# Two transformer layers on one core: where the second-stage weights are measured, and how many softmax units VectorE takes per head

## The chip, the cores and the metric

The kernel runs on one core of one Trainium2 chip. The metric is device time in microseconds, and the median of three runs of the kernel before is 1906.23 us (1905.84 to 1906.58). In this text PE is the matrix engine TensorE, DVE is VectorE, ACT is ScalarE, POOL is GpSimd and SP is SyncE.

## The reference

The input `x` has 2048 tokens of 448 features. Two layers with the same weights are run over it, and each layer is an attention block followed by a gated block, both with a layer norm ahead and a residual add behind:

```python
x = x + A(_layernorm(x))     # qkv = x @ wqkv; 16 heads of 28; softmax(q k^T * 28**-0.5) v; @ wo
x = x + B(_layernorm(x))     # h = sigmoid(x @ w_gate) * (x @ w_up); h @ w_down, 1792 hidden
x = x + A(_layernorm(x))
x = x + B(_layernorm(x))
```

All arrays are float32.

## The kernel before, in words

The kernel is one instruction stream per engine, in the order in which the program emits it; each engine takes its instructions strictly in that order and waits at the head of its queue. Matrix products use pairs of float16 numbers, a high part and the rest. To choose the power of two by which a weight is scaled before it is split so, the kernel first needs the sum of squares of that weight over all its elements.

**Projections (`project`).** Tokens are four blocks of 512. For each block, `qk` makes seven tiles of 128 rows of queries and keys (11 matmuls each, in four rotating accumulators), and `vals` makes four tiles of values. Each `qk` tile is left by ACT (high part, squares) and DVE (low part, maximum of squares), and is stored to `qk_scr` in DRAM by a DMA from the SP queue. Work of the next blocks hangs between the tiles, in lists named `fill` and `along_values`: a block is normalised (`norm`, DVE and POOL), turned in 32 x 32 pieces into a tile `xs` (`squares`, DVE), stored to DRAM (`store`), read back in another order (`gather`), and split into high and low parts (`ready`, ACT and DVE). Block 2 and block 3 go this way in layer 0.

**Attention (`attend`).** A head has 16 chunks of 128 keys, a chunk has 4 units (128 keys by 512 queries), so a layer has 1024 units. Most units are taken three at a time as a group: PE makes the scores, ACT takes the exponential of the 128 x 1536 tile in one instruction, and PE multiplies the result with the values (`mix`, some two groups later). A few units a head go another way, and are called aside: PE makes the scores in a bank of their own (`score_aside`), and DVE works out the exponential with a polynomial, ten instructions a unit. `ASIDE` gives, for one, two or three such units a head, the chunk at which each is begun and the chunk in which it is used. `FEW` gives the number of units aside for each head of layer 0; in layer 1 all heads have three. The bank that a head's asides use is the accumulator bank of the head before it: `finish` of that head (DVE turns the accumulator, divides it and splits it, six instructions) has to have read it first.

**Preparation (`Prepare`).** During the attention of layer 0, the weights of the output projection and of the gated block are put into the form that the later stages read. Steps hang behind chunks of the attention: a list of (chunk, step) pairs is worked off by `along(c)` whenever `mix` has completed chunk c. First every weight is measured: a raw tile of up to 128 x 2048 float32 comes in by DMAs from the POOL queue, and DVE squares and adds it up (`measure`, `add`). There are twelve such tiles: `o` (`wo`), four `d` (`w_down`), seven `gu` (256 columns of `w_gate` and of `w_up`). Then `sizes` sums over partitions on POOL (`partition_all_reduce`) and makes the scales on DVE. Then come the splits: `o`, seven `w` steps (`w_down`) and fourteen `g`/`u` steps, each of them a read from the POOL queue, some 14 DVE instructions, and a DMA of the result to DRAM one step later. Each step issues the read of the next tile; the raw tiles rotate through two buffers, so a read waits until the step before has read its buffer. The DVE instructions of a step are not tied to the time of their chunk, only to their place in DVE's queue.

**Buffers.** `Slots` hands out 19 large tiles first in, first out: a tile that is given back goes to the end of the list, and its next owner waits until all its former readers, DMAs included, are done.

Of the kernel before, what the change touches and what calls it, by code (L numbers as in the profile page):

```python
# [19 lines left out]
P = 128  # L20
# [44 lines left out]


ASIDE = {1: ((6, 15, 1),), 2: ((4, 10, 3), (9, 15, 1)), 3: ((4, 9, 3), (8, 13, 1), (12, 15, 2))}
FEW = "2221212111111233"


TAIL = (0, 1, 3, 2, 5, 4, 6)
# [47 lines left out]
def interleaved_layers(ctx: ExitStack, tc: tile.TileContext, x_in, wqkv, wo, w_gate, w_up,  # L119
# [591 lines left out]
    def project(layer, wq, begun):  # L711
# [109 lines left out]
        if layer == 0:  # L821
            def scaled():
                b1.xn = big.get("xn", [P, TB, D])
                for j in range(TB):
                    b1.scale(j)

            def turned(kts):
                b1.turn_banks(6, kts)
                for j in range(TB):
                    b1.turn(j)  # L830
                b1.turned_high()
                b1.turned_low()

            fill = [idle, idle, lambda: b1.norm([0, 1]), lambda: b1.norm([2, 3]), idle, scaled]
            along_values = {0: lambda: (b1.parts(), turned([0, 1])),
                            1: lambda: (turned([2, 3]), big.put(b1.xn)),
                            2: lambda: (fin(), b2.norm()),
                            3: lambda: (b2.squares(), b2.store())}
        else:
            ones_of_values()  # L840
            fill = [idle, lambda: b1.ready(0, 1), lambda: b1.ready(2, 3), b2.norm,
                    lambda: b2.squares([0, 1]), sq(2, 2, 3), b2.store]
            along_values = {0: b3.norm, 1: lambda: (fin(), sq(3, 0, 1)()), 2: b2.gather,
                            3: sq(3, 2, 3)}
# [6 lines left out]
            fill = [idle, lambda: b2.ready(0, 1), lambda: b2.ready(2, 3), b3.store]  # L851
        fin = qk(1, b1, fill, None)
        vals(1, b1, {0: b3.gather, 2 if layer == 0 else 1: fin})
        fin = qk(2, b2, [idle, lambda: b3.ready(0, 1), lambda: b3.ready(2, 3)], None)
        fin = qk(3, blks[3], [], fin)
        if layer > 0:
            big.put(*wq.qk)
        else:
# [58 lines left out]

        return values, heads, last_values

    def true_maxima(h):  # L920

        hd = HeadOperands(h, "mx")
        hd.load()
        uid[0] += 1
        mx = cpool.tile([P, NT], F32, name=f"mx_{uid[0]}", tag="mx", bufs=2)
        mp = cpool.tile([P, 4], F32, name=f"mp_{uid[0]}", tag="mp", bufs=2)
        for t in range(NT):
            for g in range(NB):
# [12 lines left out]
        nc.sync.dma_start(g_scr[h].rearrange("c (t p) -> t c p", p=P), parts)  # L941
        hd.drop()


    class Prepare:


        def __init__(self):
            nc.vector.memset(sums[:, 3:7], 0.0)
            self.part = cpool.tile([P, 2], F32, name="part", tag="part", bufs=1)  # L950
            self.raws, self.packs = big.ring(2), big.ring(2)
            self.halves, self.half = None, 0
            tiles = [("o", 0)] + [("d", j) for j in range(4)] + [("gu", j) for j in range(7)]
            order = [(self.measure, what) for what in tiles] + [
                (self.split, what) for what in tiles[:1] + [("w", p) for p in range(NP)] + [
                    (w, p) for p in range(NP) for w in ("g", "u")]]
            self.read(*tiles[0])
            self.steps = deque()
            at = 6
            for i, (do, what) in enumerate(order):  # L960
                then = order[i + 1][1] if i + 1 < len(order) else None
                self.steps.append((at, lambda do=do, what=what, then=then:
                                   self.step(do, what, then)))
                at += ((5 if what[0] == "gu" else 4) if do == self.measure else
                       {"o": 5, "w": 8}.get(what[0], 7))
                if i == len(tiles) - 1:
                    self.steps.append((at, self.sizes))
            self.steps.append((at, self.end))
            self.pack = None
# [10 lines left out]
        def read(self, kind, j):  # L980
# [12 lines left out]
            elif kind == "w":  # L993
                for z in range(2):
                    r = slice((z * NP + j) * P, (z * NP + j + 1) * P)
                    nc.gpsimd.dma_start(self.view(self.next, kind)[:, z], w_down[r])
            elif kind in "gu":
# [7 lines left out]
            else:  # L1005
                n = self.count(j)
                nc.gpsimd.dma_start(self.view(self.next, kind)[:, 0:n, :],
                                    w_down[j * 512:j * 512 + n * P, :].rearrange(
                                        "(s p) n -> p s n", p=P))

        def count(self, j):
            return min(4, NF - 4 * j)

        def view(self, t, kind):
            if kind == "gu":
# [37 lines left out]
            nc.vector.tensor_copy(sums[:, m:m + 1], self.part[:, 0:1])  # L1053

        def measure(self, raw, kind, j):
            if kind == "o":
                self.add(3, raw[:, 0:4 * D])
            elif kind == "gu":
                self.add(4, raw[:, 0:1024])
                self.add(5, raw[:, 1024:2048])  # L1060
            else:
                self.add(6, raw[:, 0:self.count(j) * D])

        def sizes(self):
            nc.gpsimd.partition_all_reduce(size[:, 3:7], sums[:, 3:7], channels=P,
                                           reduce_op=ReduceOp.add)
            powers(3, 4, size[:, 3:7])
            both_back(1, 2, 3, 2.0 ** -23)
            both_back(2, 5, 6, 2.0 ** -22)
# [767 lines left out]
```

## Time and profile before

| what | value |
|---|---|
| median of three runs | 1906.23 us |
| the profiled execution's own time | 1904.97 us |
| its span, first to last instruction | 1903.2 us |
| granted TensorE clock | 1.000 |
| PE / PE weight loads busy | 1891.3 / 1365.4 us (99% / 72%) |
| DVE / ACT / POOL busy | 1391.6 / 1386.7 / 255.9 us (73% / 73% / 13%) |
| projections of layer 0 | up to 118.7 us |
| attention of layer 0 (first to last group's start) | 119.6 to 567.3 us, 333 ACT groups |
| gated block of layer 0, projections of layer 1 | to 1062 us |
| attention of layer 1 (first to last group's start) | 1063.1 to 1506.5 us, 326 ACT groups |
| gated block of layer 1 | to the end |

PE shows as busy nearly all the time, but the ends of matmuls are modelled in the profile, so that a PE that waits a little between matmuls also shows as busy. What limits a stage has to be read from the stage itself: in attention, from whether ACT's groups stand end to end. In a row of the timeline the columns are the start in us, the duration in us, the engine, the line of the kernel, the operation, the tile written and the tiles read, the shapes, the count, and in brackets the time the engine stood idle before and what ended it.

### The profile page before, as it was taken

The numbers are of one execution on the slowest core, as the hardware profiler recorded it, in microseconds if no ns is written. First come the engines' busy times: TensorE is split into PE (matmuls) and PEld (weight loads), VectorE is DVE, ScalarE is ACT, GpSimd is POOL, SyncE is SP. The second block draws the span as 40 slices with busy tenths as digits, with TensorE's granted clock in tenths as the row PEclk, the third lists the DMA queues.
The fourth block names the chain that finished last, engine by engine and source line by source line (L and its number), as shares of the span: only waits on it lengthen the run. The fifth ranks groups of instructions, "written<-read, shape, count | busy, mean of one in ns | idle before, by whom it ended". The sixth has DMA issues, their size and how long they took to land. (4 is left out here: it accounts for less than half of the span.)

```text
span 1903.2 us, 56306 instructions
## 1 busy us (share of the span) xinstructions
PE 1891.3 (99%) x24281; PEld 1365.4 (72%) x24281; DVE 1391.6 (73%) x2768; ACT 1386.7 (73%) x1772; POOL 255.9 (13%) x523
## 2 busy tenths in 40 slices
PE   9999999999999999999999999999999999999999
PEld 4455555555556789999954568777777767899998
DVE  7648798697886688787564487787778676887664
ACT  5569999999993556555344799999999745565541
POOL 2013312232102211222100000000000021121110
PEclk9999999999999999999999999999999999999999
DMA  5575554445213565646734321122121244566553
GB/s 175 166 208 159 153 165 138 129 139 159 91 64 106 179 220 226 225 190 226 255 109 128 94 52 44 34 51 52 30 48 53 69 132 152 215 243 232 210 206 141
DMA packets 107953, 269.79 MB, mean 142 GB/s; under 512 B 12894, under 2 KB 64222, under 8 KB 107568
## 3 DMA queue, kind: packets, MB, share of 16 engines
q0 software_dynamic: 32592, 162.18, 23.8%
q1 hardware_dynamic: 74768, 103.71, 19.4%
q8 instruction: 191, 3.13, 0.7%
q14 instruction: 66, 0.54, 0.1%
q10 hardware_dynamic: 336, 0.23, 0.0%
HBM read 207.88 MB, written 50.85 MB: 136 GB/s over the span
## 5 line engine op out<-in xcount | busy, mean ns | idle before, releaser
L1177 ACT ACTIVATE prob_s<-sc 128x1536 f32<-128x1536 f32 x659 | 892.0, 1485 | 6.6 <-PE sc L1162 6.4
L1213 PE MATMUL acc<-prob_s,val_s 128*32 128x256 f32 (+3 forms) x7754 | 579.7, 383 | 0.0
L1162 PE MATMUL sc<-qp_s 114*32 114x512 f16 x7896 | 565.5, 379 | 0.0
L578 PEld LDWEIGHTS <-gu_s 128*128 128x128 f16 x4368 | 426.8, 98 | 51.3 <-issue 3.8
L1162 PEld LDWEIGHTS <-qp_s 114*32 114x32 f16 x8192 | 288.2, 95 | 192.7 <-issue 94.5
L1213 PEld LDWEIGHTS acc<-prob_s,val_s 128*32 128x32 f32 x7754 | 297.9, 110 | 115.6 <-issue 8.6
L578 PE MATMUL chain<-xwide_s,gu_s 128*128 128x256 f16 x2016 | 248.0, 273 | 3.3 <-ACT two_q L1591 1.4
L1491 PE MATMUL dnp<-dn_s,hparts_s 128*128 128x224 f16 x2016 | 225.2, 259 | 0.0
L1491 PEld LDWEIGHTS <-hparts_s 128*128 128x128 f16 x2016 | 194.0, 98 | 4.5
L1564 ACT COPY one_q<-chain 128x256 f32<-128x256 f32 x224 | 82.3, 371 | 122.5 <-PE chain L578 122.0
L1193 DVE SCALAR_TENSOR_TENSOR power_q<-power_q,expo_q 128x512 f32<-128x512 f32 x222 | 153.7, 692 | 7.6
L1580 DVE TENSOR_TENSOR one_q<-side,one_q 128x512 f32<-128x512 f32 x112 | 72.2, 686 | 106.5 <-PE side L578 103.9
L578 PE MATMUL side<-xshort_s,gu_s 128*128 128x256 f16 x1120 | 140.6, 273 | 0.0
L563 PE MATMUL qkp<-xhl_s,wqk_s 128*128 128x512 f16 x616 | 138.0, 379 | 0.7 <-DVE xhl_s L542 0.3
L1378 POOL DMA_DIRECT2D gu_s<-gu_parts x104 | 56.2, 541 | 417.5 <-PE side L578 393.4
L563 PEld LDWEIGHTS <-wqk_s 128*128 128x128 f16 x616 | 60.0, 98 | 70.2 <-ACT wqk_s L231 1.1
L1242 DVE STREAM_TRANSPOSE oturned_q<-acc 128x512 f32<-128x512 f32 x32 | 22.9, 716 | 117.4 <-PE acc L1213 117.4
L578 PE MATMUL side<-xwide_s,gu_s 128*128 128x256 f16 x672 | 91.7, 273 | 0.0
L755 ACT ACTIVATE qkhl_q<-qkp 128x512 f16<-128x512 f32 x56 | 33.2, 593 | 74.5 <-PE qkp L563 72.9
L1444 ACT CAST hparts_s<-hsums_q 128x256 f16<-128x256 f32 (+1 forms) x136 | 65.1, 494 | 29.4 <-DVE hsums_q L1456 20.4
L1213 PE MATMUL acc<-power_q,val_s 128*32 128x256 f32 (+3 forms) x278 | 86.3, 393 | 0.0
L1591 ACT ACTIVATE one_q<-one_q 128x512 f32<-128x512 f32 x56 | 35.2, 629 | 64.6 <-DVE one_q L1580 64.6
(213 smaller groups left out, 2321.3 us busy)
## 6 DMA issues: line engine op xcount, KB each, us to landing
gu_s<-gu_parts POOLq DMA_DIRECT2D x104, 800.0 KB, 5.8
dn_s<-dn_parts POOLq DMA_DIRECT2D x42, 784.0 KB, 7.5
qp_s<-qk_scr SPq DMA_DIRECT2D x96, 224.0 KB
qk_scr<-qkhl_q SPq DMA_DIRECT2D x56, 256.0 KB
gu_parts<-pack_s POOLq DMA_DIRECT2D x14, 800.0 KB, 3.8
xt_scr<-xs_s SPq DMA_DIRECT2D x48, 224.0 KB
xraw_s<-xt_scr SPq DMA_DIRECT2D x12, 768.0 KB
qp_s<-qk_scr SPq DMA_DIRECT2D x64, 112.0 KB
```

Of the source, the lines that this page charges most:

```text
L563: nc.tensor.matmul(pm, w, x, start=(i == 0), stop=(i == len(terms) - 1))
L578: nc.tensor.matmul(pm, a, x, start=(first and i == 0), stop=(i == len(terms) - 1), skip_group_check=True)
L1162: nc.tensor.matmul(ps[32 * j:32 * j + 32, :], hd.k[:, keys], hd.q[:, qb * W:(qb + 1) * W], start=True, stop=True, tile_position=(0, 32 * j))
L1177: nc.scalar.activation(prob[:, 0:n, :], ps[:, 0:n, :], AF.Exp, scale=exp_scale)
L1193: nc.vector.scalar_tensor_tensor(p, p, c[k], y, op0=ALU.add, op1=ALU.mult)
L1213: nc.tensor.matmul(acc[qb * VC:(qb + 1) * VC, s], v[:, kc % TB, h, :], probs[c * NB + qb][:, s], start=(kc == 0 and a == 0), stop=(kc == N ...
L1378: queue.dma_start(self.gu[-1][m], gu_parts[p, m])
L1444: nc.scalar.copy(to[:, :, 0], a)
L1491: nc.tensor.matmul(pm, a[:, x, t], w[:, p, y], start=(begin and n == 0 and (j == 0 or alone)), stop=(n == 2), skip_group_check=True)
L1564: nc.scalar.copy(to, pm)
L1580: nc.vector.tensor_tensor(one[m], side[m], one[m], op=ALU.add)
L1591: nc.scalar.activation(out, v, AF.Sigmoid, scale=gate_scale)
```

## The change

Half of the measuring leaves the attention of layer 0. A new class `Measure` reads six of the twelve tiles (`o`, the four `d`, the first `gu`) by the POOL queue during the values of block 0 in layer 0's projections, and adds them up on DVE behind the last three `qk` tiles of block 2 and the first three of block 3; half of the `gu` tile goes to ACT. It holds one large tile for a scrap output, and up to six for the raw tiles. `Prepare` keeps six `gu` tiles, four chunks apart (five before). POOL's sum over partitions becomes a step of its own, `reduce`, and the DVE work that uses it, `sizes`, follows six chunks later. The splits stand further apart: 10 chunks for `w` (8 before), 9 for `g` and `u` (7 before), 4 after `o` (5 before); the first split of `w` now stands at chunk 40, the last step at chunk 227, and the end at 236 (66, 213 and 220 before). `FEW` gives two units aside to every head of layer 0 but the last, which has three: 33 in all (26 before), so 991 units go to ACT, in 331 groups (998 in 333 before). Head 14 had three before and has two; heads 3, 5 and 7 to 12 had one and have two.

```diff
-FEW = "2221212111111233"
+FEW = "2222222222222223"
...
-            along_values = {0: lambda: (b1.parts(), turned([0, 1])),
-                            1: lambda: (turned([2, 3]), big.put(b1.xn)),
-                            2: lambda: (fin(), b2.norm()),
-                            3: lambda: (b2.squares(), b2.store())}
+            tell = Measure()
+            along_values = {0: lambda: (b1.parts(), turned([0, 1]), tell.read(2)),
+                            1: lambda: (turned([2, 3]), big.put(b1.xn), tell.read(2)),
+                            2: lambda: (fin(), b2.norm(), tell.read()),
+                            3: lambda: (b2.squares(), b2.store(), tell.read())}
...
-        fin = qk(2, b2, [idle, lambda: b3.ready(0, 1), lambda: b3.ready(2, 3)], None)
-        fin = qk(3, blks[3], [], fin)
+        add = tell.add if layer == 0 else idle
+        fin = qk(2, b2, [idle, lambda: b3.ready(0, 1), lambda: b3.ready(2, 3), idle, add, add,
+                         add], None)
+        fin = qk(3, blks[3], [add, add, add], fin)
...
+    class Measure:
+        def __init__(self):
+            nc.vector.memset(sums[:, 3:7], 0.0)
+            self.part = cpool.tile([P, 2], F32, name="part0", tag="part", bufs=1)
+            self.junk = big.get("junk", [P, 2048], BF16)
+            self.to_read = deque([("o", 0)] + [("d", j) for j in range(4)] + [("gu", 0)])
+            self.rows = deque()
+
+        def read(self, n=1):
+            for _ in range(n):
+                kind, j = self.to_read.popleft()
+                t = big.get("raw", [P, 2048])
+                n = {"o": 4, "d": min(4, NF - 4 * j), "gu": 0}[kind]
+                v = t[:, 0:n * D].rearrange("p (s n) -> p s n", n=D)
+                if kind == "gu":
+                    v = t.rearrange("p (w s c) -> p w s c", w=2, s=4)
+                    for i, w in enumerate((w_gate, w_up)):
+                        load_rows(v[:, i], w, 0, 2 * P, nc.gpsimd)
+                elif kind == "o":
+                    load_rows(v, wo, 0, D, nc.gpsimd)
+                else:
+                    nc.gpsimd.dma_start(v, w_down[j * 512:j * 512 + n * P, :].rearrange(
+                        "(s p) n -> p s n", p=P))
+                self.rows.append((kind, t, n * D))
+
+        def add(self):
+            kind, t, n = self.rows.popleft()
+            m, n = {"o": (3, n), "d": (6, n), "gu": (4, 1024)}[kind]
+            v = t[:, 0:n]
+            nc.vector.tensor_tensor_reduce(self.junk[:, 0:n], v, v, 1.0, sums[:, m:m + 1],
+                                           op0=ALU.mult, op1=ALU.add,
+                                           accum_out=self.part[:, 0:1])
+            nc.vector.tensor_copy(sums[:, m:m + 1], self.part[:, 0:1])
+            if kind == "gu":
+                junk = qrt.get("junk", [P, 1024], BF16)
+                nc.scalar.activation(junk, t[:, 1024:2048], AF.Square, accum_out=sums[:, 5:6])
+                qrt.put(junk)
+                big.put(self.junk)
+            big.put(t)
...
         def __init__(self):
-            nc.vector.memset(sums[:, 3:7], 0.0)
...
-            tiles = [("o", 0)] + [("d", j) for j in range(4)] + [("gu", j) for j in range(7)]
+            tiles = [("gu", j) for j in range(1, 7)]
             order = [(self.measure, what) for what in tiles] + [
-                (self.split, what) for what in tiles[:1] + [("w", p) for p in range(NP)] + [
+                (self.split, what) for what in [("o", 0)] + [("w", p) for p in range(NP)] + [
                     (w, p) for p in range(NP) for w in ("g", "u")]]
...
-                at += ((5 if what[0] == "gu" else 4) if do == self.measure else
-                       {"o": 5, "w": 8}.get(what[0], 7))
+                at += 4 if do == self.measure else {"o": 4, "w": 10}.get(what[0], 9)
                 if i == len(tiles) - 1:
+                    self.steps.append((at, self.reduce))
+                    at += 6
                     self.steps.append((at, self.sizes))
...
-        def sizes(self):
+        def reduce(self):
             nc.gpsimd.partition_all_reduce(size[:, 3:7], sums[:, 3:7], channels=P,
                                            reduce_op=ReduceOp.add)
+
+        def sizes(self):
             powers(3, 4, size[:, 3:7])
```

More of the change, by code (lines that the diff above doesn't have):

```diff
@@ L996, in read @@
                     nc.gpsimd.dma_start(self.view(self.next, kind)[:, z], w_down[r])
-            elif kind in "gu":
+            else:
                 v, w = self.view(self.next, kind), {"g": w_gate, "u": w_up}[kind]
@@ L1004, in read @@
                 nc.gpsimd.memset(v[64:P, 3], 0.0)
[L1005 to L1012, printed above, removed]
         def view(self, t, kind):
@@ L1055, in measure @@
         def measure(self, raw, kind, j):
[L1056 to L1062, printed above, removed]
-        def sizes(self):
+            self.add(4, raw[:, 0:1024])
+            self.add(5, raw[:, 1024:2048])
+        def reduce(self):
             nc.gpsimd.partition_all_reduce(size[:, 3:7], sums[:, 3:7], channels=P,
                                            reduce_op=ReduceOp.add)
+        def sizes(self):
             powers(3, 4, size[:, 3:7])
```

## The prediction

> **What bounds the kernel now.** I read the engines' busy time and the costliest groups first.
>
> ```profile
> PE 1891.3 (99%) x24281; PEld 1365.4 (72%) x24281; DVE 1391.6 (73%) x2768; ACT 1386.7 (73%) x1772; POOL 255.9 (13%) x523
> L1177 ACT ACTIVATE prob_s<-sc 128x1536 f32<-128x1536 f32 x659 | 892.0, 1485 | 6.6 <-PE sc L1162 6.4
> ```
>
> PE counts as busy throughout, but ACT's exponentials stood idle only 6.6 us over both attentions: there ACT is never let go. Which of the two sets the pace is seen by comparing the layers (the exponentials' start times, layer 0 and layer 1), and two stretches of layer 0 (busy time and count of ACT; the count has one instruction more than the steps from start to start): the first with two units aside a head, the second with one.
>
> ```profile
> L1177 ACT ACTIVATE prob_s<-sc x333: 1045/1522/1631, 119.6 to 567.3; 128x1536 f32<-128x1536 f32 x166, 128x1024 f32<-128x1024 f32 x1
> L1177 ACT ACTIVATE prob_s<-sc x326: 623/1455/1507, 1063.1 to 1506.5; 128x1536 f32<-128x1536 f32 x163
> 148.38:204.65 56.27, 56.27 (x43) 1.00 0.60 167
> 317.76:487.38 169.62, 169.53 (x127) 1.00 0.47 143
> ```
>
> Two aside: 56.27/42 = 1.340 us a group, and a head of 62/3 groups takes 27.69 us. One aside: 169.62/126 = 1.346, and 21 groups take 28.27. Layer 1 with three aside: 443.4/325 = 1.364, and 61/3 groups take 27.74. From one to two a head gains 0.58 us; from two to three nothing, since PE, which makes every unit, has become the bound (about 0.433 us a unit). Layer 0 has eight heads with one.
>
> **The change, part by part.** *Units aside.* Eight heads go from one to two: 8 x 0.58 = 4.6 us, and head 14 from three to two gives 0.05: 4.7. The layers' rows bound it otherwise: layer 1 needs 443.4 where layer 0 needs 447.7, so 4.3; by ACT's share alone seven units at 1.340/3 give 3.1. I take **4.5**, and 3.1 to 4.7 for the range.
>
> *DVE's load.* What it costs there is read from the starts of DVE's instructions in one head: `finish`, a split, a unit aside, the next split, the next `finish`, then a split of `w`, then the two halves of a `gu` measurement.
>
> ```profile
> 347.64 0.72 DVE L1242 STREAM_TRANSPOSE oturned_q<-acc 128x512 f32<-128x512 f32 x1 [6.76 <-PE acc L1213]
> 351.22 0.42 DVE L1045 TENSOR_TENSOR sums_q<-raws_s 128x256 f32<-128x256 f32 x1
> 356.99 0.75 DVE L1187 TENSOR_SCALAR expo_q<-aside,base 128x512 f32<-128x512 f32 x1
> 363.28 0.42 DVE L1045 TENSOR_TENSOR sums_q<-raws_s 128x256 f32<-128x256 f32 x1
> 375.89 0.72 DVE L1242 STREAM_TRANSPOSE oturned_q<-acc 128x512 f32<-128x512 f32 x1 [6.87 <-PE acc L1213]
> ...
> 258.76 0.38 DVE L1103 TENSOR_TENSOR sums_q<-raws_s 128x224 f32<-128x224 f32 x1
> 264.82 0.71 DVE L1242 STREAM_TRANSPOSE oturned_q<-acc 128x512 f32<-128x512 f32 x1
> ...
> 172.63 1.29 DVE L1051 CUSTOM_DVE_ANT_0 junk_s<-raw_s,sums 128x1024 bf16<-128x1024 f32 x1
> 174.18 1.28 DVE L1051 CUSTOM_DVE_ANT_0 junk_s<-raw_s,sums 128x1024 bf16<-128x1024 f32 x1
> ```
>
> `finish` 3.58, a `g`/`u` split 5.77, a unit aside 6.29, a `w` split 6.06, half a measurement 1.55. With two aside a head DVE needs 12.58 + 3.58 and its splits. At 9 chunks a split, heads 8, 9, 10, 12 and 13 have two each ahead of their `finish`, the others one: 16.16 + 11.54 = **27.70 us of 27.69**. Exactly full, and in the mean (16/9 splits) 26.4, 95%. At 10 chunks, 16.16 + 9.7 = 25.9. Who waits for DVE's queue: PE, when it makes the next head's first unit aside in the bank that `finish` must have read. How late may that be? Head 2, where `finish` waited for PE and so was on time, and where PE then made the unit:
>
> ```profile
> 179.63 0.72 DVE L1242 STREAM_TRANSPOSE oturned_q<-acc 128x512 f32<-128x512 f32 x1 [3.97 <-PE acc L1213]
> L1162 PE MATMUL aside<-qp_s x4: 378/378/379, 181.5 to 181.6; 114*32 114x512 f16 x4
> ```
>
> 181.5 - 180.35 = 1.2 us. The unit itself is used six chunks (10.4 us) and some two groups later, against 6.3 of work, so it may wait about 6: less tight. At these durations nothing is lost; I take 0.3 for `w`'s two-split heads (16.16 + 12.12 = 28.3, over by 0.6), and as ends 0 and what rival 3 works out.
>
> *Reads in the projections.* They are issued behind `b1.norm`, and `d3` and `gu` behind `b2.norm`; the last rows are POOL's queue while two `gu` tiles were read (204 to 217.5 us; the last figure is its share of the 16 DMA engines' time), and two stretches of the projections with the DMA engines' share next to last.
>
> ```profile
> 28.74 0.71 POOL L293 TENSOR_TENSOR rs<-rs,nhalf 128x2 f32<-128x2 f32 x1
> 44.04 1.02 POOL L293 TENSOR_TENSOR rs<-rs,nhalf 128x4 f32<-128x4 f32 x1
> 165.14 0.77 POOL L211 DMA_DIRECT2D raw_s<-in_B_w_gate_dram  x1 [11.35 <-DVE sums L1053]
> 168.27 0.52 POOL L214 DMA_DIRECT2D raw_s<-in_B_w_up_dram  x1
> raw_s<-in_B_w_up_dram POOLq DMA_DIRECT2D x7, 384.0 KB, 5.5
> q0 software_dynamic: 704, 2.10, 53.0%
> 40.00:50.00 10.00, 10.00 (x51) 4.73 (x49) 8.25 (x19) 4.01 (x7) 1.22 (x2) 1.00 0.01 2
> 50.00:56.00 6.00, 6.00 (x30) 2.81 (x29) 5.20 (x16) 3.20 (x6) 1.20 (x2) 1.00 0.89 185
> ```
>
> `o`, `d0` to `d2`, six DMAs of 0.5 to 0.8 us on POOL, leave from 29.5 to 33.6; `b2.norm`, which now stands behind them in POOL's queue, is wanted at 43.8, and `b3.norm` behind `gu` at 54: both free. The DMA engines are free from 40 on. The six DMAs of `gu` take POOL 3.65 us, from 45.8 (behind `d3`) to 49.5, and the large one of `w_up`, issued 1.8 us into them, lands 5.5 later, about 53. They meet block 2's store, which has the DMA engines 89% busy by itself. A `gu` tile takes 13.5 x 0.53 / 2 = 3.6 us of all DMA engines, its `w_up` half 1.8. And that store has a new follower. Counting through the list of free tiles, seven tiles fewer are free, and block 3's `xs` gets the tile that block 2's `xs` has just given back; before it got another. So DVE's first turning of block 3 waits until the store has landed (the SP queue's gather shows when: 56.6):
>
> ```profile
> 49.53 3.02 SPq L348 DMA_DIRECT2D xt_scr<-xs_s  x4
> 56.63 0.39 SPq L356 DMA_DIRECT2D xraw_s<-xt_scr  x1
> 55.97 0.65 DVE L336 STREAM_TRANSPOSE xs_s<-xn_s 128x448 f32<-128x448 f32 x1
> 60.56 0.65 DVE L756 SCALAR_TENSOR_TENSOR qkhl_q<-qkp,qkhl_q 128x512 f16<-128x512 f32 x1
> 61.44 0.35 PE L588 MATMUL vp<-wv_s,xhl_s 128*128 128x448 f16 x1
> ```
>
> 56.6 - 55.97 = 0.65 us without any contention. Behind it in DVE's queue stands the evacuation at 60.56, whose bank PE wants at 61.44 for the second value tile of block 1: 61.44 - 61.21 = 0.2 us of cover. The contention I put at the part of the `w_up` half that falls behind the store's start, 1.8 x (53.1 - 49.5)/5.5 = 1.2 us (an estimate, as if it moved evenly): 0.65 + 1.2 - 0.2 = **1.65 us** lost on PE. Ends: 0 (the store lands sooner than its gather shows, and the reads are out of the way) and 4.05 (all of `gu` still ahead of it, 0.65 + 3.6 - 0.2). The Trainium skill, "DMA: Bandwidth & Descriptors", section "Queues, rings and completion order", says that each DMA engine takes turns between queues packet by packet; no run here shows the turns, and by it the store would wait for whatever of the reads is left, between the same ends.
>
> *Adds in the projections.* Two full measurements end to end, and DVE's busy time (third) from block 2's fifth `qk` tile to block 3's last:
>
> ```profile
> 142.32 2.08 DVE L1051 CUSTOM_DVE_ANT_0 junk_s<-raw_s,sums 128x1792 bf16<-128x1792 f32 x1
> 144.63 2.08 DVE L1051 CUSTOM_DVE_ANT_0 junk_s<-raw_s,sums 128x1792 bf16<-128x1792 f32 x1
> 82.30:103.30 21.00, 21.00 (x105) 10.10 (x104) 9.21 (x22) 10.91 (x19) 0.00 (x0) 1.00 0.37 123
> ```
>
> Four adds of 2.31, half of that and a bit (1.4) for `d3`, 1.55 for half a `gu` tile: 12.2 us, against 11.8 free, and instructions that stand end to end overlap by some 0.1 us each, eight evacuations by about 1. Walked through tile by tile the backlog reaches about 6 us, while a `qk` tile's bank is wanted again after three more tiles, and is gone at the last tile. ACT's square of the other half lies in its free 10 us. So 0, and 1.0 as the upper end.
>
> *Measuring that stays.* The third `gu` tile in place of `d1`: its read waits for DVE's first measurement (142.32, the row above, + 3.1), and head 0's `finish` stands behind it.
>
> ```profile
> 150.69 2.08 DVE L1051 CUSTOM_DVE_ANT_0 junk_s<-raw_s,sums 128x1792 bf16<-128x1792 f32 x1 [3.78 <-DMA raw_s<-in_B_w_down_dram]
> 152.89 0.71 DVE L1242 STREAM_TRANSPOSE oturned_q<-acc 128x512 f32<-128x512 f32 x1
> L1162 PE MATMUL aside<-qp_s x4: 378/378/379, 154.6 to 154.6; 114*32 114x512 f16 x4
> ```
>
> 145.4 + 1.8 + 5.5 = 152.7, half a measurement 1.5, reading the bank 0.72: 154.9, against PE at 154.6: **0.3**, between 0 and 1.5.
>
> *POOL's sum.* DVE stood idle for it at the end of head 3, but that head (21 groups) took 28.33 us against the 28.27 of others with one unit aside. Taken apart: 0.
>
> ```profile
> 232.58 0.17 DVE L246 TENSOR_SCALAR pw<-size 128x4 int32<-128x4 int32 x1 [6.04 <-POOL size L1065]
> 203.39:231.72 28.33, 28.33 (x22) 1.00 0.54 150
> ```
>
> **Sum:** -4.5 + 0.3 + 1.65 + 0 + 0.3 = -2.25 us. The profiled execution took 1904.97, so 1902.7; the runs' median lies 1.26 above it, so **1904.0 us**.
>
> **The rivals.** *1, all reads hidden:* the DMA engines are free from 40 to 50 us, DVE has gaps. Then -4.5 and little else: 1901.7. Against it: the shared `xs` tile, which costs 0.45 even without contention.
>
> *2, the reads in the way:* 4.05 at the store, 1.5 at the third `gu` tile, 0.3: -4.5 + 5.85 = +1.35, 1907.6. For it: the row of 89% busy DMA engines; against it: their free stretch just before.
>
> *3, slower, DVE becomes the bound:* in two-split heads the load is 27.70 of 27.69, and slack is 1.2. Were splits and units 6% longer, heads 8 to 10 run 1.7 late each, 5.1 - 1.2 = 3.9, heads 12 and 13 3.4 - 1.2 = 2.2, and `w`'s two two-split heads (28.3 x 1.06 - 27.69 - 1.2) 1.1 each: 8.3, in place of 0.3, so -2.25 + 8.0 = +5.75, 1912.0. It eats the gain from about 3% on (0.8 a head: 1.3 + 0.4 + 0.5). A row for it: one DVE instruction of the unit aside takes up to twice its median.
>
> ```profile
> L1188 DVE TENSOR_SCALAR whole_q<-expo_q x74: 426/428/842, 127.4 to 1500.6; 128x512 f32<-128x512 f32 x74
> ```
>
> 0.4 us in 6.29 would be 6%, but the median says that it is rare. The Trainium skill, "SBUF — State Buffer", section "Who interferes with whom", holds that such DVE operations and GpSimd lock each other out for a whole instruction; the pair 428 and 842 agrees.
>
> **How the numbers follow.** A difference under 0.2% (3.8 us) is about what a measurement of this kernel cannot tell from none. Chances: forecast 0.47, rival 1 0.25, rival 2 0.15, rival 3 0.13. Faster by over 0.2% needs under 1902.4: most of rival 1 and a little of the forecast, 0.27. Slower by over 0.2% is over 1910.0: rival 3 for the most part, 0.11. The rest, 0.62, is within. The range 1901.3 to 1909.5 leaves out some 0.08 below and 0.12 above; the forecast's own is 1902.5 to 1906.0.
>
> **What would show it.** In the profile after: 331 exponentials in some 444 us from first to last; DVE's turning of block 3 waiting for a DMA at 56 to 58 us, and the first exponential 1.65 us later than 119.6; DVE 95% busy over heads 7 to 14, with `finish` seldom waiting for PE; `sizes` without idle time. The prediction is wrong if the exponentials take 447 us again, if idle time of ACT before them grows past 3 us, or if the projections end as early as before.

## The result, and the profile after

The kernel after takes 1903.08 us (median of 22 runs, 1902.06 to 1904.51), the kernel before 1906.17 us beside it (22 runs, 1904.95 to 1908.14). The ratio is 0.9984, with a 95% interval of 0.9978 to 0.9990: 3.1 us faster, which is 0.16% and so within what the prediction called no change, though the interval tells it from none. Its profiled execution took 1903.72 us with a span of 1902.0, 1.25 us less than the profiled execution of before.

First the busy line and ACT's group of the page after, then the exponentials of layer 0 and of layer 1 by their line:

```profile
PE 1888.7 (99%) x24249; PEld 1317.2 (69%) x24249; DVE 1431.1 (75%) x2835; ACT 1383.9 (73%) x1772; POOL 254.7 (13%) x523
L1213 ACT ACTIVATE prob_s<-sc 128x1536 f32<-128x1536 f32 (+1 forms) x657 | 887.6, 1484 | 7.9 <-PE sc L1198 4.3
...
L1213 ACT ACTIVATE prob_s<-sc x331: 628/1517/1578, 121.7 to 567.0; 128x1536 f32<-128x1536 f32 x165, 128x512 f32<-128x512 f32 x1
L1213 ACT ACTIVATE prob_s<-sc x326: 625/1455/1537, 1062.6 to 1505.9; 128x1536 f32<-128x1536 f32 x163
```

There are 331 groups, two fewer than before. The first starts 2.15 us later than before (121.72 for 119.57), and from the first start to the last it is 445.3 us for 447.7. Layer 1 is unchanged (443.3 for 443.4). The last group of after holds one unit where that of before holds two, and takes 0.63 us of ACT for 1.05, so up to its end the attention of layer 0 gained 2.9 us rather than 2.5. With the loss ahead of it that makes 0.8 of the 1.2 us between the two spans. The rest lies behind it: 0.6 us more are gained in the gated block of layer 1, less 0.2 that come and go elsewhere. The 0.6 is one wait of PE that the profile of before has:

```profile
1624.46 0.83 PE L578 MATMUL chain<-xwide_s,gu_s 128*128 128x256 f16 x6 [0.45 <-DVE two_q L1587]
```

PE gains this in after and in every other profile with the new list `FEW`, and does not in the one other profile with the old list (the first experiment). There is one profile of before, so whether this wait is usual there, and what the list could have to do with it, is not shown.

Where inside the attention, the busy times of two stretches show: heads 8 to 12, which had one unit aside each before and have two after (columns: the stretch and its length, then the busy time and count of PE, PEld, DVE, ACT and POOL, the granted clock, the DMA share, GB/s). The kernel before:

```profile
343.65:485.09 141.44, 141.44 (x2564) 79.22 (x2560) 113.00 (x242) 141.35 (x106) 38.88 (x67) 1.00 0.44 137
```

The kernel after, and below it heads 0, 1 and 7 to 14:

```profile
345.50:484.34 138.84, 138.84 (x2548) 83.51 (x2540) 124.93 (x247) 138.84 (x104) 30.98 (x54) 1.00 0.40 121
121.72:150.07 28.35, 28.35 (x496) 18.12 (x492) 17.75 (x31) 27.96 (x21) 6.48 (x12) 1.00 0.83 248
150.07:178.95 28.88, 27.89 (x506) 17.22 (x500) 24.34 (x45) 27.95 (x22) 12.36 (x21) 1.00 0.64 184
317.74:539.87 222.13, 222.13 (x4058) 131.70 (x4049) 202.83 (x401) 222.13 (x167) 42.72 (x74) 1.00 0.38 113
```

A head went from 141.44 / 5 = 28.29 to 138.84 / 5 = 27.77 us: 0.52. Summed over the eight heads that got a second unit, by the groups' starts, it is 4.0 us. Head 1 is the one head that became much longer: 28.88 us, with PE idle for 1.0 of them. DVE is busy for 202.83 of 222.13 us (91%) over heads 7 to 14.

The loss ahead of the attention has three parts, read from how far each PE instruction lies behind the same one of before: 0.94 us already at the first `qk` tile, 0.26 more when block 1 is turned, 0.96 more in the values of block 1. From there the 2.16 us stay constant up to the first exponential. The first part lies before anything that the change does, and the experiments show what it is.

### The profile page after: what moved, and what is told of

Its sections match the earlier page's. It is cut to its first block, busy times and chain, and to the rows that moved or that the text cites. A ratio compares the mean times of both kernels' runs of the same rounds, so it can differ in the third digit from the quotient of the medians.

```text
span 1902.0 us, 56313 instructions
## 1 busy us (share of the span) xinstructions
PE 1888.7 (99%) x24249; PEld 1317.2 (69%) x24249; DVE 1431.1 (75%) x2835; ACT 1383.9 (73%) x1772; POOL 254.7 (13%) x523
## 5 line engine op out<-in xcount | busy, mean ns | idle before, releaser
L1213 ACT ACTIVATE prob_s<-sc 128x1536 f32<-128x1536 f32 (+1 forms) x657 | 887.6, 1484 | 7.9 <-PE sc L1198 4.3
L1249 PE MATMUL acc<-prob_s,val_s 128*32 128x256 f32 (+3 forms) x7700 | 569.1, 384 | 0.0
L1198 PE MATMUL sc<-qp_s 114*32 114x512 f16 x7868 | 552.0, 379 | 0.0
L1198 PEld LDWEIGHTS <-qp_s 114*32 114x32 f16 x8192 | 268.9, 95 | 207.5 <-issue 88.6
L1249 PEld LDWEIGHTS acc<-prob_s,val_s 128*32 128x32 f32 x7700 | 268.7, 110 | 147.9 <-issue 13.2
L1229 DVE SCALAR_TENSOR_TENSOR power_q<-power_q,expo_q 128x512 f32<-128x512 f32 x243 | 168.2, 692 | 8.3
L1249 PE MATMUL acc<-power_q,val_s 128*32 128x256 f32 (+3 forms) x300 | 94.2, 396 | 0.0
```

The source lines that it names most:

```text
L1198: nc.tensor.matmul(ps[32 * j:32 * j + 32, :], hd.k[:, keys], hd.q[:, qb * W:(qb + 1) * W], start=True, stop=True, tile_position=(0, 32 * j))
L1213: nc.scalar.activation(prob[:, 0:n, :], ps[:, 0:n, :], AF.Exp, scale=exp_scale)
L1229: nc.vector.scalar_tensor_tensor(p, p, c[k], y, op0=ALU.add, op1=ALU.mult)
L1249: nc.tensor.matmul(acc[qb * VC:(qb + 1) * VC, s], v[:, kc % TB, h, :], probs[c * NB + qb][:, s], start=(kc == 0 and a == 0), stop=(kc == N ...
```

## The experiments

Every kernel is given with its difference from the kernel after, or from the one before where that is said. A ratio is to the kernel before on the same chip.

**The moved work with the old units.**

```diff
-FEW = "2222222222222223"
+FEW = "2221212111111233"
```

> The kernel after, with the units aside of the kernel before (FEW 2221212111111233 again): the moved sums, the spread splits and POOL's sum alone. My theory: the units are worth 4.1 us (the eight heads that had one went from 226.2 us together to 222.1 in the two traces), the store that block 3's turning waits for costs 0.96 us and the late third gu tile 1.2 (head 1 took 28.87 us in place of 27.69). So this kernel is slower than the one before by about 2.2 us (ratio 1.0011), and slower than the one after by 4.1. Rival A, the moved work is free or better in most executions and the 0.94 us at the start of the profiled run of after is chance: then it ties with the kernel before or beats it, and the units are worth less, about 3.1 us. Rival B, the gain comes from POOL's sum or the spread splits: then it is about as fast as after, some 3 us faster than before.

Measured: 1909.38 us against 1905.62, ratio 1.0019 (1.0010 to 1.0028). Slower than before, as my theory had it, so the units carry the gain and rivals A and B fall. But by 3.8 us in place of 2.2: the later splits now reach heads 14 and 15, which have three units aside in this list, and there DVE is too slow. The chain at 547 us, and the heads 14 and 15, which took 57.65 us together for the 55.02 of before:

```profile
546.93 0.40 PE L1249 MATMUL acc<-power_q,val_s 128*32 128x256 f32 x1 [1.34 <-DVE power_q L1232]
...
514.41:572.06 57.65, 55.83 (x1008) 38.03 (x1004) 52.46 (x95) 55.10 (x42) 1.10 (x2) 1.00 0.25 83
```

So the second unit of the middle heads is not the only thing that the new list does: it also takes a unit from head 14, which then has room for the splits that were spread into it.

**Only the units.** The kernel before, with the new list and nothing else:

```diff
-FEW = "2221212111111233"
+FEW = "2222222222222223"
```

> The kernel before with two units aside a head and nothing else: the measuring stays in the attention and the splits stay 7 and 8 chunks apart. My theory (that of rival 3 of the prediction, with the old distances): DVE needs 16.16 + 16/7 x 5.77 = 29.35 us in a head with g or u splits where ACT and PE need 27.76, and 28.28 with w splits. Heads 7 to 12 then take about 29.3 us and this kernel is slower than before by some 6 to 9 us (six heads from 28.25 to 29.35, some 6.6, less what the one unit fewer in head 14 and the earlier heads give, plus heads 13 and 14): about 1912 to 1915 us. Rival: the late splits hold nobody up, since PE's units wait long enough and the tiles are spare; then it gains the units' 4.1 us without the losses in the projections and in head 1: about 1902 us, faster than after.

Measured: 1914.62 us against 1905.62, ratio 1.0045 (1.0031 to 1.0059). The total is in the range of my theory, but the way is another. Heads 3 to 9 took 27.7 to 28.0 us each, and then head 10 took 35.7 and head 13 took 33.8. In the timeline of PE, and in the busy times of the stretches around it:

```profile
410.21 0.62 PE L1162 MATMUL aside<-qp_s 114*32 114x512 f16 x4 [4.86 <-DVE oturned_q L1242]
...
500.80 0.40 PE L1162 MATMUL aside<-qp_s 114*32 114x512 f16 x4 [4.22 <-DVE oturned_q L1242]
...
405.00:410.20 5.20, 0.35 (x8) 0.04 (x1) 5.12 (x12) 2.25 (x2) 2.77 (x5) 0.93 0.70 226
410.20:416.40 6.20, 6.19 (x52) 2.35 (x55) 5.89 (x11) 1.79 (x2) 2.96 (x6) 0.51 0.64 212
416.40:418.40 2.00, 2.00 (x48) 1.09 (x44) 1.93 (x3) 1.92 (x2) 0.00 (x0) 1.00 0.13 30
```

PE wants the bank for the next unit aside, and DVE has not yet read the last head's result out of it, because two splits stand ahead of `finish` in its queue. The starts of the two and of `finish`, for the first wait:

```profile
397.57 0.42 DVE L1045 TENSOR_TENSOR sums_q<-raws_s 128x256 f32<-128x256 f32 x1
403.35 0.43 DVE L1045 TENSOR_TENSOR sums_q<-raws_s 128x256 f32<-128x256 f32 x1
409.44 0.72 DVE L1242 STREAM_TRANSPOSE oturned_q<-acc 128x512 f32<-128x512 f32 x1
```

Until the queue is that long nothing is lost; then the loss comes as one lump. It is made worse by what the clock column shows: after 4.86 us without work PE is granted 0.51 of its clock for the next 6.2 us, and does 52 matmuls in them, 8.4 a us, where heads 8 to 12 of after hold 18.4 a us (2548 in 138.84). So 4.9 us of waiting cost 8.0 us: 6.2 us at half speed lose the other 3. The Trainium skill, "TensorE: Matmul & The Clock Gate", section "What's actually happening", says that an idle window of about 3.4 us halves the array's clock and a busy one gives it back; the runs agree (0.5 after waits of 4.2 us and more, 1.00 after the waits of 1.0 and 1.34 us), but for one stretch at the start of a profile, shown below with the kernel after again.

**Another tile for block 3's `xs`.**

```diff
-            self.junk = big.get("junk", [P, 2048], BF16)
+            self.junk = None
...
             v = t[:, 0:n]
+            self.junk = self.junk or big.get("junk", [P, 2048], BF16)
```

> The kernel after, but Measure takes its junk tile at the first add, not when it is made. One tile more is free while the blocks are turned, and block 3's xs no longer gets the tile of block 2's xs. My theory: DVE's first turning of block 3 does not wait for the store any more (1.03 us in after), PE's value tiles 4 and 5 of block 1 are 0.96 us earlier, and all that follows keeps it: 0.96 us faster than after, first exponential 1.0 us earlier. Rival: the reads of o, d and gu stand in the way of the loads themselves, or the next wait on the path (the gather of block 2 or 3) takes its place: then less than 0.3 us.

Measured: 1902.37 us against 1905.62, ratio 0.9982 (0.9973 to 0.9991). Not to be told from the kernel after. In its profile the store wait is gone: PE's shift stays at 0.23 us through the values of block 1. But 1.32 us came at another place, in the projection of block 3:

```profile
85.57 2.08 DVE L956 CUSTOM_DVE_ANT_0 junk_s<-raw_s,sums 128x1792 bf16<-128x1792 f32 x1
...
91.70 0.27 PE L737 MATMUL knorm<-sq_q,ind 128*128 128x256 bf16 x1 [1.17 <-DVE sq_q L760]
...
65.75 3.43 SPq L348 DMA_DIRECT2D xt_scr<-xs_s  x4
73.58 0.38 SPq L356 DMA_DIRECT2D xraw_s<-xt_scr  x1
```

Block 3's store left 1.2 us sooner than in after, but its gather left only at 73.58 (after: 66.94 and 73.67). So DVE began the adds no sooner than in after (85.57 and 85.35), while PE, which no longer waits at the store, was 1.9 us ahead of where it was there. The backlog of the adds, which in after ends just in time, then reaches PE. Why that one store took longer to land is not seen in the trace.

**The first measure of the attention earlier.**

```diff
-            at = 6
+            at = 4
...
-                at += 4 if do == self.measure else {"o": 4, "w": 10}.get(what[0], 9)
+                at += (4 if i else 6) if do == self.measure else {"o": 4, "w": 10}.get(what[0], 9)
```

> The kernel after, but the first gu measure of the attention stands at chunk 4 in place of 6, the others where they were. In after the read of the third gu tile of the attention waits for that measure (POOL's first issue at 147.88, its last part landed 155.6), and head 0's finish started at 157.23 behind its measurement; PE stood idle 1.0 us for the bank. My theory: the read leaves some 3.5 us earlier, the measure no longer waits, head 1 takes 27.76 us in place of 28.87: 1.1 us faster than after. Rival: the read is slow because twelve reads are queued on POOL one behind the other and the rest of the time is lost to the DMA engines; then head 1 still takes over 28.4.

Measured: 1902.16 us against 1905.62, ratio 0.9981 (0.9972 to 0.9990). In the profile of after, head 1 had lost its microsecond like this (DVE, POOL and PE):

```profile
154.17 1.28 DVE L1090 CUSTOM_DVE_ANT_0 junk_s<-raw_s,sums 128x1024 bf16<-128x1024 f32 x1 [3.30 <-DMA raw_s<-in_B_w_gate_dram]
157.23 0.71 DVE L1278 STREAM_TRANSPOSE oturned_q<-acc 128x512 f32<-128x512 f32 x1
147.88 0.78 POOL L211 DMA_DIRECT2D raw_s<-in_B_w_gate_dram  x1 [16.47 <-DVE sums L1092]
157.99 0.40 PE L1198 MATMUL aside<-qp_s 114*32 114x512 f16 x4 [0.99 <-DVE oturned_q L1278]
```

In this experiment `finish` was on time (it waited for PE), and that wait of PE is gone, as my theory had it. Yet heads 0 and 1 together took 57.23 us as in after, so the microsecond was not gained: the rival's number without its reason, for PE now stood still at another place, waiting for none of the engines:

```profile
154.72 0.72 DVE L1278 STREAM_TRANSPOSE oturned_q<-acc 128x512 f32<-128x512 f32 x1 [1.42 <-PE acc L1249]
...
151.03 0.62 PE L1249 MATMUL acc<-prob_s,val_s 128*32 128x256 f32 x8 [0.50 <-issue]
```

The read of the third `gu` tile now ran at 140 to 149 us, beside the loads of the next heads' operands, and a packet of the instruction queue q8, which I take to be PE's code, started 2.6 us later than in after (148.34 for 145.77 us). That PE ran out of instructions is my reading of "issue" and of that packet; it is not shown by an experiment that moves the code load alone. That the packet came 8.2 us behind the one before is no sign by itself: in two of the kernels below (the third measure behind `finish`, and both edits) such packets lay 8.9 and 10.4 us apart between 155 and 167 us, and PE lost nothing there.

**The kernel after again.**

> The kernel after, unchanged, on the same chip as the next three. My theory: 2.5 to 3.5 us faster than before; PE's shift at its first qk tile (17.5 us), which was -0.02 to +0.95 us in five profiled runs with the same instructions up to there, comes out at another value again; the store wait of block 3's first turning is 0.5 to 1.2 us; head 1 loses about 1.1 us. Rival: the 0.95 us at the start belongs to the kernel after and comes back with the same size.

Measured: 1902.58 us against 1905.74, ratio 0.9984 (0.9975 to 0.9994); a profiled span of 1900.9 us. At the first `qk` tile PE's shift was 0.36 us where the first profile of the same kernel had 0.94. Over ten profiled executions it was anything from -0.02 to 0.94, and 0.40 for the kernel that is the one before up to there. So this part is chance of the execution, not of the change. In the first profile of after the greater part of it arose in a stretch at half the matrix clock:

```profile
7.70:11.10 3.40, 3.37 (x14) 2.11 (x12) 2.03 (x6) 2.28 (x6) 2.95 (x11) 0.50 1.08 284
```

PE's shift grew from 0.38 to 1.04 us in this stretch. No other profile here has one at half clock before the attention, and no wait of PE ahead of it was over 1.25 us; PE had been busy for 1.60 of the 3.39 us before. The turning of block 1 (0.25) and head 1 (28.82 us) came back as they were. The loss by the store wait was 0.49 us here, and from 0.49 to 1.13 in the seven profiles in which block 3 shares the tile, 0.81 in the mean.

**The third measure behind `finish`.**

```diff
-                at += 4 if do == self.measure else {"o": 4, "w": 10}.get(what[0], 9)
+                at += (6 if i == 1 else 4) if do == self.measure else {"o": 4, "w": 10}.get(what[0], 9)
```

> The kernel after, but the third gu measure of the attention stands at chunk 16, behind head 0's finish, in place of 14, and all later steps two chunks later. Moving the first measure ahead took DVE's wait for the data away, and yet head 1 stayed at 28.78 us: PE then stood idle 0.5 us at 151.0 for no engine, while its code load (q8, usually every 5 to 7 us) had come 8.2 us behind the one before, among busy DMA engines. My theory: both are one cause, reads that crowd the DMA engines at 140 to 156 us. Here finish does not stand behind the read, so PE's wait of 1.0 us for the bank at 158 goes; the reads leave at the same times as in after, so the code loads come as there (5 to 6 us apart) and PE loses nothing to them: head 1 takes about 27.8 us and the kernel is 1.0 us faster than after. Rival: PE loses about 1 us to its code loads wherever the reads stand, as in the run before: heads 0 and 1 together again take 57.1 us or more, and the time is that of after.

Head 1 of this kernel:

```profile
149.07:176.77 27.70, 27.70 (x506) 19.75 (x500) 23.64 (x45) 27.70 (x22) 12.29 (x21) 1.00 0.71 192
```

27.70 us, 1.18 less than in after, and heads 0 and 1 took 56.05 us together, the 56.06 of before. The place of the loss is settled: it is `finish` behind a measurement whose data are late. But the time of the runs hardly moved: 1902.53 us, ratio 0.9983 (0.9974 to 0.9992), next to 1902.58 for the kernel after beside it.

**Both.** The two edits of the third and the sixth experiment in one kernel, run on two occasions:

> Both: Measure's junk tile taken at the first add, and the third gu measure behind head 0's finish. With junk taken late, block 3's turning did not wait any more, but block 3's gather left SP's queue 4.4 us behind the store's last issue in place of 3.2 to 3.3, DVE began the adds at 85.57, and PE waited 1.17 us for DVE at 91.7: the adds were not free. My theory A: the late gather was chance (one straggling packet), so here PE's shift from the first qk tile to the first exponential is only the 0.25 us of the turning, and with head 1 at 27.8 the kernel is about 2 us faster than after, 5 us faster than before (ratio 0.9973). Theory B: DVE's work has no room, and what is gained at the store is lost at the adds each time (0.9 to 1.3 us): then it is 1 us faster than after.

> The kernel of e7 once more, on another occasion. Its first profiled execution lost nothing at the store, the adds or head 1 and took 1900.8 us, but the median of its runs, 1902.45, was that of after: so in most of its executions something takes 1.7 us. Theory A: that is the late gather of block 3 and the wait for the adds, as the other run with the late junk tile showed it (PE 1.17 us for DVE at 91.7): a second profile of this kernel then shows about 1.3 us between its first qk tile and its first exponential, in place of 0.25, or 0.25 again in a lucky execution. Theory B: it is the start, where PE's first qk tile was up to 0.95 us later in some executions than in others: then the second profile shows 0.25 and a later first qk tile. Theory C: chance of eleven runs; the median of these eleven is below 1902.0.

The first profile had a span of 1899.0 us and the second 1899.7, the two shortest of all. DVE's first two turnings of block 3 in the second, in order, no wait:

```profile
56.92 0.65 DVE L336 STREAM_TRANSPOSE xs_s<-xn_s 128x448 f32<-128x448 f32 x1
58.00 0.65 DVE L336 STREAM_TRANSPOSE xs_s<-xn_s 128x448 f32<-128x448 f32 x1
```

In both profiles only the 0.25 us of the turning lies between the first `qk` tile and the first exponential, and head 1 took 27.79 and 27.77 us. Nothing was lost at the adds, so of the first two theories A had the places right. But the medians were 1902.45 (ratio 0.9984, 0.9975 to 0.9993) and 1902.90 us (0.9981, 0.9972 to 0.9990): that of after, both times, in runs that spread from 1900.8 to 1904.9, so in time both of those theories missed. Of the theories for the second occasion, C falls. Between A (late gathers and the adds, as in the third experiment) and B (the start) the second profile speaks a little for B, with a first `qk` tile at 0.55 us in place of -0.02, but both profiled executions were the fastest of their eleven runs. What takes some 1.5 us in the usual one is open. No kernel here is shown to beat the one after.

**The old distance of the splits.**

```diff
-                at += 4 if do == self.measure else {"o": 4, "w": 10}.get(what[0], 9)
+                at += 4 if do == self.measure else {"o": 5, "w": 8}.get(what[0], 7)
```

> The kernel after with the splits at the old distances: o 5, w 8, g and u 7 chunks in place of 4, 10 and 9. With two units aside in every head and the old distances the kernel before lost 4.86 us of PE at 410 and 4.22 us at 501 us, each time one wait for the bank that finish had not yet read, behind two splits. My theory: the same here, since it follows from the distance alone: two lumps of 6 to 8 us, in heads that have three splits or two late ones, so 10 to 15 us slower than after, about 1914 to 1918 us. Rival: the stall came from the longer measuring in the attention of that kernel and not from the distance; here, with half the measuring gone, the heads stay at 27.8 us and the time is that of after.

One run: 1917.05 us, 14.5 us more than the kernel after beside it. PE in the timeline:

```profile
355.65 0.62 PE L1198 MATMUL aside<-qp_s 114*32 114x512 f16 x4 [5.01 <-DVE oturned_q L1278]
...
445.56 0.62 PE L1198 MATMUL aside<-qp_s 114*32 114x512 f16 x4 [5.04 <-DVE oturned_q L1278]
```

Heads 8 and 11 took 34.4 and 35.5 us, the others from head 2 to head 14 took 27.7 to 27.8. The same two lumps, with half the measuring gone: the distance of the splits is enough for them.

**POOL's sum and its use together again.**

```diff
                     self.steps.append((at, self.reduce))
-                    at += 6
                     self.steps.append((at, self.sizes))
```

> The kernel after with POOL's sum and its use in one step again (the six chunks between them taken out, so the splits come six chunks earlier). My theory (the forecast's 0 for this part): DVE idles some 6 us for POOL at about 190 us, with two units aside in that head PE has room of over 6 us before it uses the unit queued behind, and no head becomes longer than 27.8: the span is that of after within 1 us. Rival: with two units aside the idle time of DVE is no longer to be had; the next finish comes late, PE waits for its bank, and a head near 190 us takes 1 us or more longer than 27.76.

One run: 1912.74 us with a span of 1911.0, 9.0 us above after's first profile. My theory was wrong here. DVE, and PE, which wants the bank that `finish` (the transpose) still holds; then the stretches of the wait and behind it:

```profile
187.40 0.17 DVE L246 TENSOR_SCALAR pw<-size 128x4 int32<-128x4 int32 x1 [5.93 <-POOL size L1098]
191.06 0.71 DVE L1277 STREAM_TRANSPOSE oturned_q<-acc 128x512 f32<-128x512 f32 x1
191.82 0.62 PE L1197 MATMUL aside<-qp_s 114*32 114x512 f16 x4 [7.84 <-DVE oturned_q L1277]
...
184.00:191.82 7.82, 0.00 (x0) 0.00 (x0) 4.32 (x9) 1.68 (x2) 2.60 (x4) 0.84 0.22 59
191.82:196.00 4.18, 4.17 (x44) 2.13 (x47) 3.97 (x8) 1.31 (x1) 1.23 (x3) 0.50 0.85 291
```

POOL's sum takes 6 us from DVE's last addend to DVE's first use, and head 1's `finish` stands behind it. Head 2 took 37.9 us. In the kernel after, the same instruction of DVE comes at 192.78 without idle time, behind a unit aside.

## Why the prediction was right, step by step

The median came out 0.9 us below the forecast of 1904.0, and no rival happened. The nearness of the number is in part luck, as the sum below shows. The terms fared like this.

*Units aside, -4.5.* The mechanism is the one told, and the size -4.0: a head with two took 27.77 us where 27.69 was forecast. The lower figure came from a stretch of two heads of before. Head 14 did not gain 0.05 but lost 0.15. The gain needs the rest of the change, though, which the sum did not say: with the splits at the old distances it turns into a loss against before (9.0 us without the rest of the change, 11.3 with it), and with POOL's sum undivided into one of 6.6.

*`w` heads with two splits, +0.3.* They lost nothing. Five times DVE worked 27.8 to 28.6 us from one `finish` to the next without a wait, more than the 27.76 of a head, and was late within what the bank allows: at the closest, behind head 10, 0.85 us were left between the end of DVE's reading of the bank (433.88) and PE's next use of it (434.73).

*Store and turning, +1.65.* Place and mechanism as told: DVE's turning of block 3 at 58.30 us waits for the store, and PE's values behind it are late.

```profile
58.30 0.65 DVE L336 STREAM_TRANSPOSE xs_s<-xn_s 128x448 f32<-128x448 f32 x1 [1.03 <-DMA xt_scr<-xs_s]
50.84 3.49 SPq L348 DMA_DIRECT2D xt_scr<-xs_s  x4
58.28 0.38 SPq L356 DMA_DIRECT2D xraw_s<-xt_scr  x1
...
q0 software_dynamic: 172, 0.48, 21.6%
```

The size was 0.96 here and 0.81 in the mean of seven profiles. What was too large is the contention of 1.2: from the store's first issue to the gather it took 7.44 us, against 7.10 before, so 0.3 (and 7.22 in the mean of the ten profiles with the reads beside it, so 0.1), although the last row (51 to 58 us) shows that the reads did have a fifth of the DMA engines in that time. The forecast had let all that was left of the read's `w_up` half delay the store by its full length; the store went on beside it. Of the cover of 0.2 only 0.07 was there: PE lost 0.96 of DVE's 1.03.

*The turning of block 1, not forecast, +0.25.* Line 319's four instructions before, and after:

```profile
L319 DVE TENSOR_SCALAR xn_s<-x,mv,rs x4: 507/507/507, 32.6 to 33.9; 128x448 f32<-128x448 f32 x4
```

```profile
L319 DVE TENSOR_SCALAR xn_s<-x,mv,rs x4: 495/504/774, 33.6 to 35.1; 128x448 f32<-128x448 f32 x4
```

One of the four takes 774 ns in place of 507 while POOL issues its reads, PE's turning stands behind it, and that is the 0.25 to 0.26 us that all profiles with the moved reads show and none without them. The prediction looked at what stands behind the reads in POOL's queue (rightly free), not at DVE beside it. The Trainium skill, "SBUF — State Buffer", section "Who interferes with whom", which the prediction cited for another line, holds for this one: it names such operations of DVE as ones that can shut POOL out, or be shut out, for a whole instruction.

*Adds, 0.* Right for the kernel after, and just so. DVE from 82 to 103 us:

```profile
82.00:103.00 21.00, 21.00 (x104) 10.01 (x103) 20.64 (x42) 13.19 (x24) 0.00 (x0) 1.00 0.30 101
```

20.64 of 21.00 us, and PE lost nothing. The third experiment shows the edge: with DVE some 2 us later against PE, 1.17 us of PE are gone, which is past the 1.0 that was given as the upper end.

*The third `gu` tile, +0.3.* The right place, but 1.2 in place of 0.3. The read left at 147.88 where the sum had 145.4, which is 0.3 more than the 2.15 us by which the whole attention starts later. It took 8.0 us to the end of DVE's wait for its second half (155.84), where 1.8 + 5.5 = 7.3 were assumed. The two add 1.0 to the 0.3.

*POOL's sum, 0.* Right as a difference from before; wrong as a judgment of what it does. It was costed in a head with one unit aside. With two, the undivided sum costs 9 us.

*The sum.* -4.0 + 0.15 + 0.25 + 0.81 + 0 + 1.2 = -1.6 us from the profiles, against -2.25 forecast, and -3.1 (-4.2 to -1.9, by the interval) in the medians. Errors of both signs cancelled. The medians show about 1.5 us more than these places account for. Of that 0.2 lies in other heads of the attention, and 0.6 would be the wait at 1624 us, if before has it in most executions; the rest is not explained.

*The rivals.* 1 (all reads hidden) did not happen: the store and the third `gu` tile are seen on the path. 2 (4.05 us at the store) neither. 3 did not happen here, but the runs with closer splits show that it was close, and that its price was worked out the wrong way: it is not so much per late head, but nothing up to a point and then 6 to 8 us at once, the clock included.

Of the signs that were named, the 331 groups took 445.3 us in place of 444 (the difference is head 1), the first exponential came 2.15 us later in place of 1.65, and ACT's idle time before the exponentials of layer 0 went from 3.4 to 4.3 us; the turning waited at 57.3 to 58.3 us, `finish` waited for PE behind only four of heads 7 to 14 (7, 8, 11 and 14, and behind 8 for just 0.26 us; behind 9, 10, 12 and 13, to which the prediction gave two splits, not at all), `sizes` had no idle time, and DVE was busy for 91% where 95 were forecast.

## What to carry to other kernels

When an engine off the critical path is filled to the brim, the question is not its share but which of its instructions holds something that the bound engine wants (here the read of a bank), and how much work may stand ahead of that one: up to there extra work is free, beyond it the loss comes in one piece and here the halved matrix clock made it 29 to 64% larger. So distances between background steps are worth as much as the gain that they make possible, and should be priced with the load that will be there, not with that of the kernel before. Changes of 1 us in a kernel of 1900 can be located in a profile, but these runs could not tell them apart in time, and the same instructions started up to 1 us apart from execution to execution.

## What was not expected of the hardware

- With each of the five waits of PE of 4.2 to 7.8 us came a stretch of 3.4 or 6.8 us at half the granted clock (0.50 and 0.51 in the rows above). A wait of 4.86 us thereby cost 8.0, and one of 7.84 cost 10.1; in all five the loss was the wait and half of the half-clock time behind it, within 0.2 us.
- POOL's sum over partitions of a 128 x 4 tile shows as 0.4 to 0.9 us of POOL in the profiles, yet DVE got its result 6 us after its last addend (181.4 to 187.4 us).
- One DVE `tensor_scalar` of 128 x 448 went from 507 ns to 762 to 774 beside POOL's DMA issues, in all ten profiles with the moved reads.
- PE stood still 0.50 us at 151 us for no engine in one kernel, when a packet of the instruction queue was late among busy DMA engines; that the one caused the other is not shown.
